# Attention and two feed-forward blocks on one core: the copies of the rounded q and k made by DMA, q's remainder made by POOL, first loads on two queues, new orders

## The chip, the core and the metric

The kernel runs on one core of a Trainium2 chip. The core has TensorE (PE, matrix products), VectorE (DVE), ScalarE (ACT), GpSimd (POOL) and SyncE (SP). Each engine works through its own instructions in the order in which they were written, and waits for the others by semaphores. PE reads its operands from on-chip memory (SBUF) and writes to a small accumulator memory (PSUM); DVE and ACT read both, POOL only SBUF. DMAs are issued by SP and by ACT. The metric is the device time of one execution, in microseconds (us).

## The reference

Four batches of eight heads, 576 positions, 64 elements in a head. Attention with a decay bias is followed by two feed-forward blocks; the change is in attention.

```python
scores = scale * np.matmul(q, k.transpose(0, 1, 3, 2))
cum = np.cumsum(np.maximum(s, 0.0), axis=-1)
bias = -(cum[:, :, :, None] - cum[:, :, None, :])
scores = np.where(causal, -1000000000.0, scores + np.minimum(bias, 0.0))
scores = scores - np.max(scores, axis=-1, keepdims=True)
attn = np.exp(scores)
attn = attn / (np.sum(attn, axis=-1, keepdims=True) + 1e-09)
attn_out = np.matmul(attn, v)
# x = attn_out, heads side by side; then
# block 1: relu(x @ w_in) = (u, v); v normalised over its elements;
#          (u * (w_spatial @ v + b_spatial)) @ w_out
# block 2: mixes of x with its shifted copy; sigmoid(xr @ w_r) * (relu(xk @ w_k)^2 @ w_v)
```

## The kernel before

The 32 heads are worked on in 16 pairs. Products of full precision are made of rounded parts: an operand is split into a rounded part and a remainder, and the products of these parts are added up. For q and k of a pair, `st_T` (line 360) does this: `first` casts the raw tile into the rounded part (items `wh` for q, `xh` for k), a second copy of that rounded part goes to other partitions (`ud` for q, `vd` for k), and `second` subtracts it from the raw tile for the remainder (`ul`, `vl`). Four tiles hold the result: W and X with the rounded parts on partitions 64 to 127, beside the bias rows and the maxima on partitions 0 to 3 and up; U and V with a rounded part on one half of the partitions and a remainder on the other. All are parts of one tile, so the profile calls them `big`; the raw q and k are `qk`.

`st_S` (line 393) multiplies W by X for approximate scores and takes their maxima on DVE (tile `s`, twelve products and twelve reductions for a pair, items `s0` to `s11`); `Ma` and `Mb` transpose the maxima on PE, copy them on ACT (`mt`) and send them by DMA into W. `st_E` (line 434) computes the scores with V, U and X, W (tile `ps`, items `e0` to `e9` and `ez`), exponentiates them on ACT, and blanks what lies above the diagonal on POOL (the selects of line 467). `st_V` (line 489) multiplies by v and by a column of ones (tile `pv`, items `a0` to `a4` and `b0` to `b4`); ACT copies the sums out (`fa`, `fb`, tile `pt`, line 516). The normalisation goes by DMA: `n1` sends the row of sums to a 128-partition tile (`r<-pt`), `n2` takes the reciprocal on DVE and sends it to DRAM (`rd<-r`), `n2b` loads it back onto 64 partitions (`rb<-rd`), and `n30` and `n31` multiply (line 538), one on DVE and one on POOL.

A step p (`step`, line 619) does E of pair p, V of pair p-1, S of pair p+1, T of pair p+2 and the end of the normalisation of pair p-2. The items of all these are carried out in the order of the table `ORDER` (line 549); items named in `LATE` are left for the next step. Each engine gets its instructions in that order. Between the items stand parts of the decoding of the later weights (`dL` loads, `dF` on ACT, `dD` on DVE and POOL, `dT` on ACT and POOL, `dS` stores). Each `ldq` and `ldk` loads q or k of a later pair. The tables `START` (line 606) and `TAIL1`, `TAIL2` (lines 878 and 882) do the same for pairs 0 to 2 and for the end of attention with the start of the first block. `ENGINE` (line 111) says which engine does an item (V is DVE, S is ACT, P is POOL), `QUEUE` (line 114) which DMAs go by ACT ("A"); the others go by SP. A DMA waits on SP until its source is ready, and all SP's later DMAs wait behind it.

Pairs 0 to 2 have entries of their own with the prefixes A, B and C; pairs 3 to 15, which steps 1 to 13 split, use the entries without a prefix:

```python
wh="S", xh="S", ud="S", vd="S", ul="V", vl="V"
```

Of the kernel before, what the change touches and what calls it, by code (L numbers as in the profile page):

```python
# [25 lines left out]
def tile_kernel(  # L26
# [560 lines left out]
    def ones():  # L587
# [3 lines left out]
        for t in VT:  # L591
# [15 lines left out]
    START = """ldk0 ldq0 lds ldk1 cx0 mask cw0 sums 0xh0 bases cx1 ldq1 sums2 0wh0 0ul0 dL 0wh1 rx00 dL 0ul1 augd pads0  # L607
               0xh1 pads1 1wh1 rx01 tiny 0ud0 s0 s5 0ud1 s3 1wh0 s10 dL 1ud0 cx2 dF s1 ldq2 cw1 1rows dD 1xh1 0vd0 1ud1
               s9 0vl0 dT s2 s8 2rows dF s4 1ul1 pads2 1xh0 s6 dL s11 1s0 s7 0vd1 1s4 dS 1ul0 2wh0 dF cw2 2wh1 dD Ma
               lv0 0vl1 1s6 2ud0 ldk2 1s3 1s10 lv1 e0 2ul0 Mb e1 e3 ltv0 2ul1 2xh0 2xh1 1vd1 1vd0 1s2 1s1 2vd1 e4 e2  # L610
               1vl1 1s7 ldq3 ldq4 1s9 2vl1 1s11 1s5 e5 1s8 ones 1Ma 1vl0 e7 ldk3 1Mb e6 2vd0 e8 e9 ez 2vl0 2ud1"""
# [266 lines left out]
    TAIL1 = """V1 e0 e3 va0 dF va1 e1 va2 WV e5 va3 va4 un2 vfa dT un2b vb0 vb1 e6 dD WS dF e4 dF dD vb2 vb3 dT vb4 vfb
               dF dT dT e2 un31 dS e8 g0 wa0 wa1 ez dF g0s dT vn1 dF wa2 e9 wa3 e7 g0c un30 wa4 dL wfa dL g1 wb0 wb1
               g0r WU wb2 dD wb3 dL wb4 vn2 dL wfb vn2b wn1 g1s dF dT g2 g3 dD g1c dS g2s dF g3s wn2 vn30 dS g1r dT dD  # L880
               g4 dL dF vn31 wn2b dD g3c g2c wn31 dD wn30"""
    TAIL2 = """dT dT dF dT q4 dD p1 dF g4s p0 dL dT q1 p0s g4c p1s g4r g3r B0 g2r dT dT q7 q3 q2 p2 p2s dL p3 p4 dD dF
               p4s q6 p3s q0 dD dS dS dS dF q5"""
# [195 lines left out]
```

## Time and profile before

| | |
|---|---|
| median of 3 runs | 686.35 us |
| lowest and highest run | 684.46 and 687.14 us |
| span of the profiled execution (no other time is given for it) | 684.9 us |
| busy: PE, DVE, ACT, POOL | 650.0, 504.3, 375.6, 341.8 us |
| mean of a step from 49.4 to 188.0 us (twelve steps) | 11.55 us |

The span is counted from the first to the last instruction of one profiled execution; it lies 1.45 us below the median of the runs. Start of attention, the steps and its tail take the first 263 us; after that PE works nearly without a gap. In a row of the profile, `out<-in` names the tile that is written and the tile that is read; a bracket at the end says how long the engine was idle before, and what ended that. A "q" behind an engine's name (SPq, ACTq) is its queue of DMA issues; such a row's duration is that of the issue, not of the transfer.

### The profile page before, as it was taken

The numbers are of one execution on the slowest core, as the hardware profiler recorded it, in microseconds if no ns is written. First come the engines' busy times: TensorE is split into PE (matmuls) and PEld (weight loads), VectorE is DVE, ScalarE is ACT, GpSimd is POOL, SyncE is SP. The second block draws the span as 40 slices with busy tenths as digits, with TensorE's granted clock in tenths as the row PEclk, the third lists the DMA queues.
The fourth block names the chain that finished last, engine by engine and source line by source line (L and its number), as shares of the span: only waits on it lengthen the run. The fifth ranks groups of instructions, "written<-read, shape, count | busy, mean of one in ns | idle before, by whom it ended". The sixth has DMA issues, their size and how long they took to land.

```text
span 684.9 us, 10966 instructions
## 1 busy us (share of the span) xinstructions
PE 650.0 (95%) x3640; PEld 558.0 (81%) x3640; DVE 504.3 (74%) x1038; ACT 375.6 (55%) x824; POOL 341.8 (50%) x490
## 2 busy tenths in 40 slices
PE   2599999999999979999999999999999999999998
PEld 1476666666757968998999999988989898898987
DVE  6878887878853687768858754479596877959773
ACT  5599999999975474575565453331423323142330
POOL 4445656565674646566567555442434344244430
PEclk9999999999999989999999999999999999999999
DMA  6645556564458627562364572721001010000101
GB/s 180 131 107 151 156 144 161 143 164 128 123 158 264 210 72 222 158 198 94 101 208 146 150 260 84 258 111 47 0 1 47 0 47 1 31 17 1 46 1 47
DMA packets 65065, 78.23 MB, mean 114 GB/s; under 512 B 28763, under 2 KB 45563, under 8 KB 64496
## 3 DMA queue, kind: packets, MB, share of 16 engines
q1 hardware_dynamic: 63674, 75.81, 37.0%
q10 hardware_dynamic: 1334, 1.72, 1.0%
q8 instruction: 28, 0.46, 0.3%
q14 instruction: 29, 0.24, 0.1%
HBM read 54.05 MB, written 21.79 MB: 111 GB/s over the span
## 4 chain that ended last, share of the span: by engine, by line
PE 78%; DMA 9%; ACT 7%; DVE 4%; issue 1%; POOL 0%; ACTq 0%; SPq 0%; DVEq 0%
PE mm L703 57%; PE mm L788 8%; PE pv L505 4%; DMA r<-pt 3%; PE ps L443 3%; DMA qk<-in_qk_dram 2%; ACT big L105 2%; ACT pt L516 2%; PE pv L502 2%; DMA rd<-r 1%; PE s L405 1%; ACT e L463 1%; PE pv L501 1%; DVE jk L411 1%; DMA big<-augd 1%
## 5 line engine op out<-in xcount | busy, mean ns | idle before, releaser
L703 PE MATMUL mm<-big 128*128 128x384 f32 (+2 forms) x1176 | 202.5, 332 | 0.0
L703 PEld LDWEIGHTS mm<-big 128*128 128x128 f32 x1176 | 191.3, 188 | 8.6
L703 PE MATMUL mm<-w,vb 128*128 128x512 f32 (+1 forms) x304 | 90.4, 381 | 0.0
L986 DVE TENSOR_TENSOR r<-r 128x384 f32<-128x384 f32 x48 | 53.7, 1119 | 46.6 <-ACT r L983 46.6
L443 PE MATMUL ps<-big 128*128 128x288 f32 (+3 forms) x320 | 84.0, 362 | 1.7 <-ACT e L463 0.8
L405 PE MATMUL s<-big 128*128 128x288 f32 (+3 forms) x192 | 61.9, 378 | 20.4 <-POOL big L108 12.3
L145 POOL TENSOR_TENSOR f<-f,raw 128x256 int32<-128x256 int32 x64 | 53.4, 834 | 43.9 <-DVE f L143 33.7
L411 DVE CUSTOM_DVE_ANT_0 jk<-s,mask 128x288 bf16<-128x288 f32 (+4 forms) x160 | 61.9, 429 | 16.2 <-PE s L405 13.9
L467 POOL TENSOR_SCALAR_AFFINE_SELECT e<-e 128x128 f32<-128x128 f32 x128 | 52.4, 419 | 42.0 <-ACT e L463 37.2
L443 PEld LDWEIGHTS ps<-big 128*128 128x128 f32 x320 | 55.3, 197 | 19.8 <-issue 12.1
L405 PEld LDWEIGHTS s<-big 128*128 128x128 f32 x192 | 36.3, 206 | 36.6 <-DVE mx L411 12.6
L463 ACT ACTIVATE e<-ps 128x288 f32<-128x288 f32 (+3 forms) x160 | 60.6, 418 | 8.5 <-PE ps L443 7.1
L703 PEld LDWEIGHTS mm<-w,vb 128*128 128x128 f32 x304 | 56.0, 188 | 11.2
L788 PE MATMUL mm<-ws,vb 128*128 128x288 f32 x384 | 59.3, 303 | 4.6 <-DVE ws L120 2.6
L505 PE MATMUL pv<-e,vp 128*65 128x448 f32 (+2 forms) x192 | 63.5, 436 | 0.0
L1006 DVE RECIPROCAL rr<-rr 128x512 f32<-128x512 f32 x18 | 60.4, 3353 | 0.6
L788 PEld LDWEIGHTS mm<-ws,vb 128*128 128x128 f32 x384 | 54.8, 194 | 5.6 <-DVE ws L120 3.4
L987 ACT CAST vb<-r 128x384 fp32r<-128x384 f32 x48 | 24.7, 515 | 56.9 <-DVE r L986 56.9
L729 POOL TENSOR_TENSOR gh<-mix,vb 128x384 fp32r<-128x384 f32 x24 | 25.5, 1070 | 52.3 <-ACT vb L728 49.7
L703 PE MATMUL mm<-gh,wo 128*128 128x288 f32 x256 | 51.3, 294 | 0.0
L729 POOL TENSOR_TENSOR big<-mix,big 128x384 fp32r<-128x384 f32 x24 | 25.9, 1083 | 47.4 <-ACT big L728 38.7
L120 DVE TENSOR_TENSOR big<-qk,big 64x1152 fp32r<-64x1152 f32 (+1 forms) x37 | 44.3, 1201 | 6.1 <-ACT big L105 4.9
(126 smaller groups left out, 1289.1 us busy)
## 6 DMA issues: line engine op xcount, KB each, us to landing
qk<-in_qk_dram SPq DMA_DIRECT2D x28, 288.0 KB
out_dram<-rr SPq DMA_DIRECT2D x17, 256.0 KB
rb<-rd SPq DMA_DIRECT2D x15, 288.0 KB
raw<-in_moe_w_in_dram SPq DMA_DIRECT2D x16, 256.0 KB
vp<-in_v_dram SPq DMA_DIRECT2D x16, 256.0 KB
raw<-in_moe_w_k_dram SPq DMA_DIRECT2D x16, 256.0 KB
raw<-in_moe_w_v_dram SPq DMA_DIRECT2D x16, 256.0 KB
big<-d_wk SPq DMA_DIRECT2D x8, 512.0 KB
```

The costliest lines, as they stand in the source:

```text
L145: nc.gpsimd.tensor_tensor(out=f, in0=f, in1=low, op=ALU.add)
L405: nc.tensor.matmul(out=ps[:, 0:kn], lhsT=W[g][:, h, 128 * i:128 * i + 128], rhs=X[g][:, x0:x0 + kn], start=True, stop=True,)
L411: nc.vector.tensor_tensor_reduce(out=jk[r0:128, 0:kn], in0=ps[r0:128, 0:kn], in1=mask[r0:128, m0:m0 + kn], scale=1.0, scalar=(dst if mid e ...
L443: nc.tensor.matmul(out=ps[:, o:o + b - a], lhsT=st[g][:, key0(h, 128 * j):key0(h, 128 * j) + 128], rhs=mv[g][:, h, 64 + a:64 + b], start=( ...
L463: nc.scalar.activation(out=e[:, o:o + n], in_=ps[:, 0:n], func=ACTF.Exp, scale=scale)
L467: nc.gpsimd.affine_select(out=d, in_=d, pattern=[[1, w]], base=0, channel_multiplier=-1, compare_op=ALU.is_ge, fill=0.0,)
L505: nc.tensor.matmul(out=pv[0:VW, 1, 448 - w:448], lhsT=lt, rhs=e[:, OFF[j]:OFF[j] + w] if j < 4 else es[p][:, w * h:w * h + w], start=False ...
L703: nc.tensor.matmul(out=ps, lhsT=x, rhs=y, start=(m == 0), stop=(m == n - 1))
L729: nc.gpsimd.tensor_tensor(out=dst[1][:, kc, :], in0=t, in1=dst[0][:, kc, :].bitcast(F32), op=ALU.subtract)
L788: nc.tensor.matmul(out=o, lhsT=x[:, sc, dd], rhs=y[:, sc, t], start=(sc == 0 and m == 0), stop=False)
L986: nc.vector.tensor_tensor(out=r, in0=r, in1=r, op=ALU.mult)
L1006: nc.vector.reciprocal(out=r, in_=r)
```

## The change

For pairs 3 to 15, `ud` and `vd` become DMAs on SP's queue. For q, ACT still casts into W and the DMA copies W's rounded part to U. For k, ACT now casts into V, on the partitions of the raw tile, and the DMA copies V's rounded part to X, which S reads; `vl` then needs the cast alone. `vd` is no longer in `LATE`, so it is issued in the step of the cast. q's remainder `ul` goes from DVE to POOL. k of pair 0 and q of pair 1 are loaded by SP's queue instead of ACT's, and the second maxima of pair 0 go by ACT's. `START`, `ORDER`, `TAIL1` and `TAIL2` are written in new orders; they hold the same items as before.

```diff
-    ENGINE = dict(... wh="S", xh="S", ud="S", vd="S", ul="V", vl="V", ...)
+    ENGINE = dict(... wh="S", xh="S", ud="D", vd="D", ul="P", vl="V", ...)
...
-    QUEUE = dict(lds="P", ldq0="A", ldk0="A", ..., ldq1="A", ldk1="A", ..., Mb="P", ...)
+    QUEUE = dict(lds="P", ldq0="A", ldk0="P", ..., ldq1="P", ldk1="A", ..., Mb="A", ...)
...
+        def moved(nm):
+            return ENGINE[f"{pre}{'ud' if nm == 'q' else 'vd'}{0 if len(heads) > 1 else ''}"] == "D"
+
         def first(nm, i, eng):
-            COPY[eng](hi(nm, i), raw(nm, i))
+            COPY[eng]((dup if nm == "k" and moved("k") else hi)(nm, i), raw(nm, i))
...
+        def again(nm, i, eng):
+
+            a, b = dup(nm, i), hi(nm, i)
+            if not moved(nm):
+                COPY[eng](a, b.bitcast(F32))
+            elif nm == "k":
+                nc.sync.dma_start(out=b.bitcast(F32), in_=a.bitcast(F32))
+            else:
+                nc.sync.dma_start(out=a.bitcast(F32), in_=b.bitcast(F32))
...
-                items[d + e] = lambda i=i, nm=nm, key=pre + d + e: COPY[ENGINE[key]](
-                    dup(nm, i), hi(nm, i).bitcast(F32))
+                items[d + e] = lambda i=i, nm=nm, key=pre + d + e: again(nm, i, ENGINE[key])
...
-    ORDER = """s4 s0 s3 wh zero lv s6 ul x1 e0 rows xh a0 dT n2 e1 a1 s1 n2b ltv s5 a2 s11 a3 dD vd x0 e2 s10 a4 s2 fa
+    ORDER = """x4 s4 wh x2 s0 ltv s3 dT e0 e1 s6 ul e2 dD lv n2 dL rows s1 a0 s2 a2 a1 x1 s11 xh s5 e4 a3 vd a4 n2b
...
-    LATE = "vd vl"
+    LATE = "vl"
```

SP's queue in the middle of the attention steps, from one rd to the next rb, before. Line 528 is rd, 534 rb, 124 a load of the decoding and 158 its store, 426 the maxima, 278 a load of q or k, 521 r, 357 the zeroed row, 284 v, 352 the bias rows.

```order
L528 DMA rd<-r_1417 128x9
L534 DMA rb<-rd 64x1152
L124 DMA raw<-in_moe_w_in_dram 128x256
L158 DMA d_wv<-hl_86 256x1x256
L426 DMA big<-mt 1x5x128
L278 DMA qk_137<-in_qk_dram 64x1152
L426 DMA big<-mt 1x5x128
L521 DMA r_1582<-pt 128x1x9
```

The same stretch of SP's queue after the change, from rd to r. Lines are 12 to 14 higher; 392 is the copy of k, 394 the copy of q.

```order
L540 DMA rd<-r_1419 128x9
L124 DMA raw<-in_moe_w_in_dram 128x256
L352 DMA big<-augd 3x1152
L392 DMA big<-big 64x1152
L546 DMA rb<-rd 64x1152
L357 DMA big<-big 1x16x80
L438 DMA big<-mt 1x5x128
L158 DMA d_wv<-hl_86 256x1x256
L394 DMA big<-big 64x2x576
L278 DMA qk_137<-in_qk_dram 64x1152
L438 DMA big<-mt 1x5x128
L533 DMA r_1584<-pt 128x1x9
```

Between rd and rb now stand a load, the bias rows and the copy of k; between rb and r stand six DMAs, among them the copy of q, where five stood.

POOL in the middle of the attention steps, before: the decoding (lines 120 and 145), the selects, the multiplication by rb (538), the selects of the last block (481, 484).

```order
L467 AFFINE_SELECT e<-e 128x128 x2
L120 TENSOR_TENSOR hl_86<-f,hl_86 128x256
L145 TENSOR_TENSOR f<-f,raw 128x256
L467 AFFINE_SELECT e<-e 128x128 x6
L538 TENSOR_TENSOR x_72<-pt,rb 64x576
```

POOL after the change, the same stretch, with q's subtraction as the line with `64x2x576`.

```order
L120 TENSOR_TENSOR hl_85<-f,hl_85 128x256
L479 AFFINE_SELECT e<-e 128x128
L120 TENSOR_TENSOR big<-qk_137,big 64x2x576
L479 AFFINE_SELECT e<-e 128x128
L145 TENSOR_TENSOR f<-f,raw 128x256
L479 AFFINE_SELECT e<-e 128x128 x6
L550 TENSOR_TENSOR x_72<-pt,rb 64x576
```

q's subtraction stands between the first two selects of a step, behind the decoding's subtraction and ahead of its addition.

## Rows read from the trace of the kernel before

**Rows 1.** The page, first part: busy us, share of span, instructions.

```profile
PE 650.0 (95%) x3640; PEld 558.0 (81%) x3640; DVE 504.3 (74%) x1038; ACT 375.6 (55%) x824; POOL 341.8 (50%) x490
```

**Rows 2.** By step: us, busy PE, PEld, DVE, ACT, POOL; clock, DMA share, GB/s.

```profile
118.40:130.00 11.60, 11.12 (x61) 7.84 (x60) 9.34 (x32) 11.18 (x23) 6.67 (x14) 1.00 0.54 145
...
sum 138.60, PE 134.19 PEld 94.69 DVE 116.12 ACT 132.50 POOL 80.81; mean PE 11.18 PEld 7.89 DVE 9.68 ACT 11.04 POOL 6.73
```

**Rows 3.** Chain of waits: start us, us, what. PE's rate without disturbance, two places.

```profile
123.28 0.75 PE pv L502 x2
...
299.47 1.58 PE mm L788 x12
```

**Rows 4.** Chain of waits in two steps.

```profile
116.27 3.73 DMA r<-pt
120.02 0.21 DVE r L526
...
127.25 0.64 ACT pt L516
...
128.11 1.83 DMA r<-pt
```

**Rows 5.** SP's queue in order of time: start us, us of issue, line.

```profile
116.27 0.51 SPq L521 DMA_DIRECT2D r<-pt  x1
...
120.31 0.35 SPq L528 DMA_DIRECT2D rd<-r  x1
122.69 0.47 SPq L534 DMA_DIRECT2D rb<-rd  x1
...
128.11 0.51 SPq L521 DMA_DIRECT2D r<-pt  x1
```

**Rows 6.** Groups by shape, eight steps: count | busy, mean ns | idle before.

```profile
L120 DVE TENSOR_TENSOR big<-qk,big 64x1152 fp32r<-64x1152 f32 x17 | 23.3, 1373 | 2.1 <-ACT big L105 1.8
L105 ACT CAST big<-big 64x1152 fp32r<-64x1152 f32 x16 | 18.4, 1153 | 0.4
...
L411 DVE CUSTOM_DVE_ANT_0 jk<-s,mask 128x448 bf16<-128x448 f32 x16 | 9.3, 619 | 0.0
...
L538 DVE TENSOR_TENSOR x<-pt,rb 64x576 f32<-64x576 f32 x8 | 6.1, 762 | 3.5 <-DMA rb<-rd 3.3
```

**Rows 7.** Line 120 by engine: ns min/median/max, first and last start, shapes.

```profile
L120 POOL TENSOR_TENSOR big<-qk,big x1: 1407/1407/1407, 16.9 to 16.9; 64x576 fp32r<-64x576 f32 x1
```

**Rows 8.** In order of time, POOL's two, then DVE's two beside them.

```profile
106.72 1.04 POOL L467 TENSOR_SCALAR_AFFINE_SELECT e<-e 128x128 f32<-128x128 f32 x1 [0.50 <-ACT e L463]
...
115.24 1.92 POOL L538 TENSOR_TENSOR x<-pt,rb 64x576 f32<-64x576 f32 x1
...
106.25 1.35 DVE L120 TENSOR_TENSOR big<-qk,big 64x1152 fp32r<-64x1152 f32 x1 [0.22 <-ACT big L105]
...
115.13 0.75 DVE L538 TENSOR_TENSOR x<-pt,rb 64x576 f32<-64x576 f32 x1 [1.08 <-DMA rb<-rd]
```

**Rows 9.** Chain of waits: a load of 64 rows, 288 KB, to its landing.

```profile
91.17 4.10 DMA qk<-in_qk_dram
```

**Rows 10.** Start of the kernel in order of time, POOL, DVE, ACT, PE.

```profile
5.18 0.72 POOL L108 TENSOR_SCALAR big<-qk 64x576 fp32r<-64x576 f32 x1 [1.50 <-DMA qk<-in_qk_dram]
...
7.01 0.75 DVE L335 TENSOR_TENSOR big<-e,big 32x576 fp32r<-32x576 f32 x1
...
9.00 0.67 ACT L105 CAST big<-qk 64x576 fp32r<-64x576 f32 x1 [2.40 <-DMA qk<-in_qk_dram]
9.42 1.32 ACTq L342 DMA_DIRECT2D big<-big  x1
...
12.26 3.40 PE L405 MATMUL s<-big 128*128 128x288 f32 x8 [12.26 <-POOL big L108]
```

**Rows 11.** By stretch, columns as in group 2: end of attention.

```profile
200.00:220.00 20.00, 18.64 (x89) 12.92 (x89) 5.99 (x17) 10.04 (x24) 11.50 (x23) 1.00 0.83 260
...
240.00:260.00 20.00, 15.40 (x92) 14.37 (x91) 16.18 (x29) 14.62 (x33) 8.49 (x10) 0.83 0.23 69
```

More of the change, by code (lines that the diff above doesn't have):

```diff
@@ L110, in tile_kernel @@
     COPY = {"V": vcopy, "S": scopy, "P": pcopy}
-    ENGINE = dict(n30="V", dH="S", dO="P", n31="P", xe0="P", xe1="V", xe2="P", xe3="P", xe4="P", gl0="P", gl1="V", gl2="P", gl3="V", cw0="V", cx0="S", cw1="D", cx1="S", cw2="V", cx2="D", bs="V", N130="V", N131="V", N140="P", N141="V", N150="V", N151="V", wh="S", xh="S", ud="S", vd="S", ul="V", vl="V", Awh0="S", Axh0="P", Aud0="P", Avd0="S", Aul0="V", Avl0="P", Awh1="S", Axh1="V", Aud1="P", Avd1="S", Aul1="V", Avl1="V", Bwh0="S", Bxh0="S", Bud0="P", Bvd0="S", Bul0="V", Bvl0="V", Bwh1="P", Bxh1="S", Bud1="S", Bvd1="P", Bul1="V", Bvl1="V", Cwh0="P", Cxh0="S", Cud0="S", Cvd0="V", Cul0="V", Cvl0="V", Cwh1="S", Cxh1="S", Cud1="S", Cvd1="P", Cul1="V", Cvl1="V", ph0="S", pl0="V", ph1="S", pl1="V", ph2="S", pl2="V", ph3="S", pl3="V", ph4="S", pl4="V")
-    QUEUE = dict(lds="P", ldq0="A", ldk0="A", ltq0="A", ltk0="P", ldq1="A", ldk1="A", rx00="A", rx01="P", augd="A", Ma="P", Mb="P", n13="A", d13="P", b13="P", n14="P", d14="A", b14="P", n15="A", d15="A", b15="A")
+    ENGINE = dict(n30="V", dH="S", dO="P", n31="P", xe0="P", xe1="V", xe2="P", xe3="P", xe4="P", gl0="P", gl1="V", gl2="P", gl3="V", cw0="V", cx0="S", cw1="D", cx1="S", cw2="V", cx2="D", bs="V", N130="V", N131="V", N140="P", N141="V", N150="V", N151="V", wh="S", xh="S", ud="D", vd="D", ul="P", vl="V", Awh0="S", Axh0="P", Aud0="P", Avd0="S", Aul0="V", Avl0="P", Awh1="S", Axh1="V", Aud1="P", Avd1="S", Aul1="V", Avl1="V", Bwh0="S", Bxh0="S", Bud0="P", Bvd0="S", Bul0="V", Bvl0="V", Bwh1="P", Bxh1="S", Bud1="S", Bvd1="P", Bul1="V", Bvl1="V", Cwh0="P", Cxh0="S", Cud0="S", Cvd0="V", Cul0="V", Cvl0="V", Cwh1="S", Cxh1="S", Cud1="S", Cvd1="P", Cul1="V", Cvl1="V", ph0="S", pl0="V", ph1="S", pl1="V", ph2="S", pl2="V", ph3="S", pl3="V", ph4="S", pl4="V")
+    QUEUE = dict(lds="P", ldq0="A", ldk0="P", ltq0="A", ltk0="P", ldq1="P", ldk1="A", rx00="A", rx01="P", augd="A", Ma="P", Mb="A", n13="A", d13="P", b13="P", n14="P", d14="A", b14="P", n15="A", d15="A", b15="A")
     def queue(key):
@@ L548, in tile_kernel @@
     late = {}
-    ORDER = """s4 s0 s3 wh zero lv s6 ul x1 e0 rows xh a0 dT n2 e1 a1 s1 n2b ltv s5 a2 s11 a3 dD vd x0 e2 s10 a4 s2 fa
-               e4 x2 e5 dL s8 e3 s7 b0 ud dS vl Ma dF b1 e8 s9 e7 e6 ldk n30 n31 b2 b3 Mb b4 fb ez n1 e9 x3 ldq x4""".split()
-    LATE = "vd vl"
+    ORDER = """x4 s4 wh x2 s0 ltv s3 dT e0 e1 s6 ul e2 dD lv n2 dL rows s1 a0 s2 a2 a1 x1 s11 xh s5 e4 a3 vd a4 n2b
+               zero fa s8 e5 e3 s10 e9 Ma b0 vl s7 s9 e8 dS ud e7 n31 b2 dF ldk b3 ez Mb b1 n30 b4 fb x3 n1 x0 e6
+               ldq""".split()
+    LATE = "vl"
     def run(*stages):
@@ L606, in tile_kernel @@
                   for key in ("cw0", "cx0", "cw1", "cx1", "cw2", "cx2")})
[L607 to L611, printed above, removed]
+    START = """tiny cw0 pads1 lds ldq0 sums ldk0 cx0 0xh0 bases 0wh0 pads0 ldk1 cx1 dL sums2 rx00 mask ldq1 1wh1
+               rx01 0ul0 0ud0 dL 0xh1 0wh1 0ul1 s0 cx2 ldq2 s5 s6 0ud1 augd dF dL 1rows s1 s3 0vd0 1ud1 1xh1 dD cw1
+               s7 s8 lv1 s10 0vd1 0vl0 2wh0 s2 s4 s9 dT 1wh0 dF 1ul1 2wh1 1xh0 s11 dS 0vl1 1s0 1s6 dD cw2 Ma ldk2
+               1s3 1ud0 dL 1vd0 1s10 e0 dF e3 pads2 2xh0 1ul0 e1 2xh1 1s2 2ud0 2ul1 Mb 2ul0 ldq4 1vd1 2rows 2vd1
+               lv0 1vl1 1s7 e4 ltv0 ones e2 1s1 1s4 1s8 1s5 ldq3 e5 1s9 2vd0 1Ma e7 1s11 e8 2vl0 2vl1 e9 1Mb 1vl0
+               2ud1 ez ldk3 e6"""
     for nm in START.split():
@@ L877, in tile_kernel @@
     })
[L878 to L883, printed above, removed]
+    TAIL1 = """e0 dF V1 va0 va3 va2 e1 va1 WV un2 va4 e5 vfa dT dF vb0 e9 vb3 vb1 dD un2b dT vb2 ez e4 vb4 dF vfb
+               e6 e8 dT dT un30 WS g0 wa0 e2 dD e3 un31 wa1 dF vn1 g0s dT e7 wa2 wa3 wa4 dL dF dS dL g0c wfa vn2 g1
+               g0r WU wb0 wb1 dL wb3 wb2 g1s wb4 dF wfb dF dT wn1 g2 vn2b g3 g1c dD dD dF g2s wn2 g3s dD dS g1r g4
+               wn2b vn31 vn30 dL dF dT g3c dS dD g2c wn31 dD dL wn30"""
+    TAIL2 = """dT dD dT g4s dD dT p0 dF dT p0s q3 p1 dL q4 g4c g2r p1s g4r q0 dT g3r q7 B0 p2 p2s p3 p4 p3s q2 p4s
+               dF q6 dS dL dF q1 dD dF dS dS q5 dT"""
     for nm in TAIL1.split():
```

## The prediction

> **What bounds the kernel now.** I read the page first. PE is busy for 95% of the span [rows 1], but its ends are modelled, so I looked for the stretches in which it does less than it could. The busy times by stretch show two: the first 40 us, and the attention steps from 49 to 188 us. Those are twelve steps in 138.6 us, 11.55 us each, and one step has 11.04 us of ACT work, 9.68 of DVE and 6.73 of POOL [rows 2]. ACT is full to 96%, so it is the first thing that sets a step.
>
> How low could PE go? Twelve products of 288 columns take 1.58 us where nothing disturbs them, 0.457 ns a column; a value product of 448 columns takes 0.75 us, 1.674 ns a column [rows 3]. A step has 6,400 columns of the scores that are exponentiated (E) and 3,200 of the scores for the maxima (S) at the first price, 3,200 of values and 256 of transposes at the second: 4.39 + 5.36 + 0.43 = 10.2 us. That is PE's floor; 1.35 us a step is lost.
>
> The chain of waits tells the rest. From 116 to 128 us it runs: the DMA r<-pt that takes 3.73 us, DVE's reciprocal at 120.02, DVE and PE work, ACT's copy of the second head's sums at 127.25, and the next r<-pt at 128.11 [rows 4]. So there is a second limit beside ACT: the normalisation goes through DMAs, and DVE, which works in order, stands at the reciprocal until the first has landed. SP shows the whole ring: r at 116.27, rd at 120.31, rb at 122.69, the next r at 128.11 [rows 5]. DVE's multiplication by rb also waits, 3.3 us over eight steps [rows 6].
>
> **The change part by part.**
>
> 1. *ACT loses two copies a step.* Each is 1.153 us [rows 6]. 11.04 - 2 x 1.153 = 8.73 us a step. ACT no longer sets the step.
>
> 2. *DVE loses q's subtraction*, 1.373 us [rows 6]: 9.68 - 1.37 = 8.31 us. k's stays.
>
> 3. *POOL gains it.* The trace has one POOL subtraction of this kind, 64x576 in 1.407 us [rows 7]; twice that is 2.81 us for 64x1152 (an estimate). 6.73 + 2.81 = 9.54 us a step, so POOL goes from the idlest engine to one that is nearly full. Its selects are used half a step to a step later, which covers a lag of a few us.
>
> 4. *POOL and DVE hold each other up.* At 115.24 POOL began a multiplication that took 1.92 us; the same shape took 1.41 elsewhere. DVE had begun a two-input operation at 115.13, which ended at 115.88. At 106.72 a POOL select began that took 1.04 us; DVE's subtraction ran from 106.25 to 107.60, and the select ended 0.16 us later [rows 7, 8]. So one waits for the other to end. The subtraction that moves held POOL for 1.37 us a step; now it can hold DVE for 2.81. In the new order it stands on POOL beside DVE's three decode operations, and the reciprocal stands right behind these. Bounds: from 0 (DVE's three come first; no gain, since POOL's selects have their cover) to 2.81 us a step (POOL's comes first each time). I take 0.3, about one meeting of the size of rows 8 (0.5 us) in every second step, because the two go by turns there, and keep both ends.
>
> The Trainium skill, "SBUF — State Buffer", section "Who interferes with whom", states this as a rule that speaks against the change: a DVE instruction with two SBUF inputs and a GpSimd instruction that reads SBUF exclude each other for a whole instruction, whichever starts first. By that rule a collision costs DVE up to the full POOL subtraction, where sums per engine would cost nothing: the step would be 10.7 us by the sums, 674 us in all, and 12.5 us with half of the subtraction in DVE's way, 697 us in all. The two meetings of rows 8 agree with the rule.
>
> 5. *Two DMAs a step go onto SP's queue*, 288 KB each. An issue takes some 0.5 us of SP, and SP has waits to absorb it; twelve issues become fourteen. A load of that size and row length landed 4.10 us after its issue [rows 9]. The copy of k is needed by the first score product of the next step. k's cast ends on ACT some 4.5 us into the step (an estimate: q's and k's cast at 1.15, four or five short operations ahead of it at about 0.4), the DMA is issued by 5.6 and lands by 9.7, 1.3 us before an 11.0 us step ends. That is its cover; what it slips beyond that, PE waits. The copy of q has a whole step. Bytes: 1.7 MB a step now, 2.3 after, 206 GB/s over 11.0 us; 260 GB/s was moved from 200 to 220 us [rows 11]. So it fits, but a DMA waits more often behind another: 0 to 1 us on the ring r, rd, rb.
> Queued behind k's copy, which waits for ACT, stand rb, the zero row and the maxima, so DVE and POOL, which wait for rb, wait for it too. As rb waits for rd to land anyway (2.4 us between their issues [rows 5]), the raw load, the rows and k's copy lie in that gap.
>
> 6. *The new order* puts DVE's three decode operations ahead of the reciprocal where q's subtraction stood. The chain of rows 4, worked out anew: copy 0.64 and 0.2 to r's issue (both from 127.25 to 128.11), r 3.73, reciprocal 0.21, two score reductions until PE gets a buffer, 1.1 (the widest is 0.62 [rows 6]), then PE's remaining work of the step: 4,640 columns at 0.457 ns, 1,600 + 256 at 1.674 ns, 5.2 us. Sum 11.1 us. In every second step r took only some 1.8 us in the chain (1.83 at 128.11 [rows 4]), and PE's floor holds, 10.2 to 10.4. Mean 10.7; with 0.3 from point 4, **11.0 us a step** against 11.55.
>
> 7. *First loads.* ACT's first cast of q waited until 9.00 us for its load, issued behind k's on the same queue; the rows' DMA stood behind it at 9.42, and PE began at 12.26. k's load, issued first, was there at 5.18 [rows 10]. With q first on ACT and k on SP, the rows' DMA waits only for DVE's sums, ready at 7.76, and goes out 1.6 us earlier. DVE is busy for most of the rest of the start, so later reorderings give little. Bounds 0 to 3 us; I take 1.5.
>
> 8. *The tail's orders.* PE loses 4.6 us between 240 and 260, with a mean granted clock of 0.83 of the full 2.4 GHz [rows 11], in a run of small ACT, DVE and POOL steps that are only reshuffled. Nothing in the trace says which way; between -3 and +3, taken as 0.
>
> **Sum.** The changed copies lie in thirteen steps: 13 x (11.55 - 11.0) = 7.2, and 1.5 from the start: 8.7 off the profiled span of 684.9 us gives 676.2. The median of the runs is 1.45 above that span: **678 us**.
>
> **The rivals.**
> - *PE's floor is reached.* r's landing and the port cost nothing more, as ACT's late copies were what delayed the sums: 10.3 us a step, 13 x 1.25 + 1.5 = 17.8, 668.6 us. For it: ACT is at 96%. Against it: DVE's waits for DMAs in rows 4 and 6, which are not ACT's.
> - *The ring of r, rd and rb stays as long as it is.* 0.4 us more on it from DMAs behind one another, and a step takes 11.5: 13 x 0.05 + 1.5, 684 us. For it: in rows 5 the time from r to r is 11.84 us, and six issues besides r itself now stand between rb and the next r where five stood.
> - *Slower: POOL's subtraction gets in ahead of DVE's decode.* It decides whether POOL's operation starts before DVE's third one. Then DVE stands for up to 2.81 us ahead of the reciprocal, half of it on average, 1.4: 11.1 + 1.4 = 12.5 us a step, 13 x 0.95 = 12.4 more, less 1.5: 697 us. For it: rows 8, and the rule named above. Against it: the two take turns there, and POOL has three shorter operations to do first.
>
> **How the numbers follow.** Forecast 0.45, floor 0.15, ring unchanged 0.24, slower 0.16. One measurement can tell 0.5%, 3.4 us, from no change: below 682.9 is faster, above 689.8 slower. Faster: 0.40 of the forecast's, 0.15 of the floor's and 0.02 of the ring's, 0.57. Within: 0.25. Slower: 0.15 of the last and 0.03 of the ring's if the tail goes wrong too, 0.18. The range takes in the floor case with its start (667) and reaches into the slower case up to 693: less than 0.2 is left out. The likeliest case alone, with start and tail at their bounds, is 673 to 683.
>
> **What would show it.** In the steps from 49 to 188 us: ACT at some 8.7 us a step, POOL at 9.5, two DMA issues more, and a step of 11.0. Point 4 shows as DVE decode operations that last until POOL's subtraction ends; point 5 as PE waiting at the first score product for big<-big; the ring as idle time of DVE before the reciprocal and before the multiplication by rb; point 7 as PE's first product near 10.7 us. The prediction is wrong if a step is under 10.5 or over 11.5 us, or if the time moves outside attention by more than 4 us.

## The result and the profile after

The changed kernel takes 691.15 us against 686.61 us measured beside it (twelve runs each), a ratio of 1.0054 with an interval of 1.0028 to 1.0080: half a per cent slower. The profiled execution has a span of 689.4 us; before it was 684.9. Step times come from one profiled execution each, and runs of one kernel differ by some 1% (the changed kernel's lie from 686.5 to 694.4 us): of the experiments below, e8's profile is of its slowest run (695.8 us, median 690.3) and e9's of its fastest (678.0, median 683.7).

| stretch | before | after | difference |
|---|---|---|---|
| first score product begins | 12.26 us | 10.88 us | -1.4 |
| first reciprocal of the steps | 50.18 us | 51.89 us | +1.7 |
| mean of the next eleven steps | 11.58 us | 12.19 us | +0.61 each, +6.8 |
| end of the tail: PE begins the first product behind batch 0's spatial part | 263.05 us | 267.78 us | +4.7 |

A step is counted from one reciprocal of DVE to the next; the twelfth stands 8.5 us later than before, so some 3.8 us come back in the tail. The page of the changed kernel, busy time of each engine, the main DMA queue, and the costliest group with a wait (count, busy, mean, idle time ahead of it):

```profile
PE 646.6 (94%) x3640; PEld 558.9 (81%) x3640; DVE 495.3 (72%) x1025; ACT 344.8 (50%) x798; POOL 387.5 (56%) x503
...
q1 hardware_dynamic: 66816, 84.07, 43.9%
...
L417 PE MATMUL s<-big 128*128 128x448 f32 (+3 forms) x192 | 69.3, 413 | 30.7 <-DMA big<-big 22.6
```

PE does the same 3640 products. The 22.6 us that its score products wait for a DMA big<-big are not all of the steps: 10.9 us are the kernel's beginning (the first product at 10.88 us; before, it waited 12.3 us for POOL there), 2.9 a wait at 20 us, and 8.8 belong to the steps. These 8.8 are new. The queue's packets take 43.9% of the sixteen DMA engines' span; in the profile of before it was 37.0%. By step (columns as in [rows 2]), one step and the sum over eleven:

```profile
112.90:125.50 12.60, 10.83 (x58) 8.12 (x56) 8.42 (x30) 8.91 (x21) 10.33 (x15) 0.90 0.94 194
...
sum 134.10, PE 120.89 PEld 88.18 DVE 94.83 ACT 96.84 POOL 108.84; mean PE 10.99 PEld 8.02 DVE 8.62 ACT 8.80 POOL 9.89
```

Against [rows 2]: ACT 8.80 us a step where it had 11.04, DVE 8.62 for 9.68, POOL 9.89 for 6.73, just as the parts of the change say. But a step became longer and the DMA engines, at 0.54 in the step shown before, are at 0.94 here. The mean granted clock of this step is 0.90; what stood ahead of that is told below. The groups of eight steps, which answer to [rows 6, 7]:

```profile
L120 POOL TENSOR_TENSOR big<-qk,big 64x1152 fp32r<-64x1152 f32 x8 | 21.2, 2650 | 0.7
...
L550 POOL TENSOR_TENSOR x<-pt,rb 64x576 f32<-64x576 f32 x8 | 15.4, 1931 | 13.1 <-DMA rb<-rd 7.3 <-ACT e L475 4.2 <-ACT pt L528 1.6
...
L550 DVE TENSOR_TENSOR x<-pt,rb 64x576 f32<-64x576 f32 x8 | 6.0, 751 | 17.8 <-DMA rb<-rd 17.8
...
L143 DVE SCALAR_TENSOR_TENSOR f<-raw,g 128x256 int32<-128x256 int32 x7 | 5.4, 773 | 0.6
...
L417 PE MATMUL s<-big 128*128 128x192 f32 x16 | 4.6, 290 | 6.6 <-DMA big<-big 5.4 <-DMA big<-mt 1.2
```

The multiplications by rb wait 17.8 us on DVE, where [rows 6] had 3.3, and 7.3 us on POOL. The chain of waits through two steps shows who is late (start, length, what):

```profile
101.39 2.42 DMA rd<-r
...
103.83 0.49 SPq L546
...
104.37 4.76 DMA big<-big
...
109.17 0.65 PE s L417 x3
...
115.05 0.53 SPq L546
...
115.95 5.73 DMA big<-big
...
121.82 0.63 PE s L417 x3
```

In both steps it goes from rb's issue (line 546) through a DMA big<-big issued right behind it, 4.76 and 5.73 us, to PE's first score product (109.17 and 121.82). SP's queue names that DMA; it answers to [rows 5]:

```profile
113.12 0.36 SPq L540 DMA_DIRECT2D rd<-r  x1
...
114.43 0.51 SPq L392 DMA_DIRECT2D big<-big  x1
115.05 0.53 SPq L546 DMA_DIRECT2D rb<-rd  x1
115.95 0.57 SPq L357 DMA_DIRECT2D big<-big  x1
...
120.56 0.55 SPq L533 DMA_DIRECT2D r<-pt  x1
```

Line 392 is the copy of k, line 357 the zero row of W. PE's wait at 121.82 is for the zero row: a few kilobytes, issued at 115.95 behind rb, landing 5.7 us later. In the kernel before nobody waited for that line. In the changed kernel (us, times):

```profile
  PE s L417: 8.8, 8
  PEld s L417: 3.3, 3
```

This is the reading that the chain by names alone would have hidden: the copy of k and the zero row have the same name.

Such a wait can be followed by more than its own length. PE's row at the end of the second one:

```profile
121.82 0.63 PE L417 MATMUL s<-big 128*128 128x192 f32 x3 [1.76 <-DMA big<-big]
```

PE had done next to nothing from 120 to 122 us (0.24 us busy), and from 123 to 126 us the granted clock is 0.50 of full speed, 1.2 GHz. It is the one such stretch in the steps of the changed kernel (the wait of 1.86 us that ends at 73.21 us has none behind it); in the steps of the kernel before there is none.

### The profile page after: what moved, and what is told of

It reads as the page before. It is cut to its first block, busy times and chain, and to the rows that moved or that the text cites. A ratio compares the mean times of both kernels' runs of the same rounds, so it can differ in the third digit from the quotient of the medians.

```text
span 689.4 us, 11078 instructions
## 1 busy us (share of the span) xinstructions
PE 646.6 (94%) x3640; PEld 558.9 (81%) x3640; DVE 495.3 (72%) x1025; ACT 344.8 (50%) x798; POOL 387.5 (56%) x503
## 3 DMA queue, kind: packets, MB, share of 16 engines
q1 hardware_dynamic: 66816, 84.07, 43.9%
## 4 chain that ended last, share of the span: by engine, by line
PE 81%; DMA 10%; DVE 3%; ACT 2%; issue 1%; POOL 1%; SPq 0%; ACTq 0%; DVEq 0%; POOLq 0%
PE mm L717 56%; PE mm L802 8%; PE pv L517 5%; PE ps L455 5%; DMA big<-big 4%; DMA r<-pt 3%; PE s L417 3%; PE pv L514 2%; DMA big<-mt 1%; PE pv L513 1%; DMA rd<-r 1%; DMA augd<-big 1%; PE mm L804 1%; PE mm L803 1%; ACT big L105 1%
## 5 line engine op out<-in xcount | busy, mean ns | idle before, releaser
L417 PE MATMUL s<-big 128*128 128x448 f32 (+3 forms) x192 | 69.3, 413 | 30.7 <-DMA big<-big 22.6
L455 PE MATMUL ps<-big 128*128 128x288 f32 (+3 forms) x320 | 70.6, 332 | 5.1 <-DMA big<-mt 4.1
L423 DVE CUSTOM_DVE_ANT_0 jk<-s,mask 128x320 bf16<-128x320 f32 (+4 forms) x160 | 63.9, 427 | 15.3 <-PE s L417 14.2
L145 POOL TENSOR_TENSOR f<-f,raw 128x256 int32<-128x256 int32 x64 | 55.2, 863 | 23.2 <-DVE f L143 9.0
L517 PE MATMUL pv<-e,vp 128*65 128x192 f32 (+2 forms) x192 | 61.9, 433 | 0.7 <-POOL e L479 0.7
L479 POOL TENSOR_SCALAR_AFFINE_SELECT e<-e 128x128 f32<-128x128 f32 x128 | 50.9, 418 | 15.3 <-ACT e L475 14.0
L455 PEld LDWEIGHTS ps<-big 128*128 128x128 f32 x320 | 51.9, 197 | 7.9 <-DMA big<-mt 4.6
L1004 POOL TENSOR_TENSOR big<-r,vb 128x384 fp32r<-128x384 f32 x30 | 30.4, 1013 | 32.0 <-ACT vb L1001 26.5
```

What stands on the lines that cost most here:

```text
L145: nc.gpsimd.tensor_tensor(out=f, in0=f, in1=low, op=ALU.add)
L417: nc.tensor.matmul(out=ps[:, 0:kn], lhsT=W[g][:, h, 128 * i:128 * i + 128], rhs=X[g][:, x0:x0 + kn], start=True, stop=True,)
L423: nc.vector.tensor_tensor_reduce(out=jk[r0:128, 0:kn], in0=ps[r0:128, 0:kn], in1=mask[r0:128, m0:m0 + kn], scale=1.0, scalar=(dst if mid e ...
L455: nc.tensor.matmul(out=ps[:, o:o + b - a], lhsT=st[g][:, key0(h, 128 * j):key0(h, 128 * j) + 128], rhs=mv[g][:, h, 64 + a:64 + b], start=( ...
L479: nc.gpsimd.affine_select(out=d, in_=d, pattern=[[1, w]], base=0, channel_multiplier=-1, compare_op=ALU.is_ge, fill=0.0,)
L517: nc.tensor.matmul(out=pv[0:VW, 1, 448 - w:448], lhsT=lt, rhs=e[:, OFF[j]:OFF[j] + w] if j < 4 else es[p][:, w * h:w * h + w], start=False ...
```

## The experiments

Ratios are to the kernel before, run beside each; "step" is the mean of the eleven steps after the first reciprocal, from the profiled execution. In runs of the kernel before's steps (its own profile and three of the runs below) that mean is 11.58 to 11.77 us.

### Undoing one part in the steps

The first theory was that PE waits because the copies are late. Each of four runs sets back one entry of the engine table:

```diff
-ud="D", vd="D", ul="P"
+ud="D", vd="S", ul="P"    # e1: k's copy back on ACT
+ud="S", vd="D", ul="P"    # e2: q's copy back on ACT
+ud="S", vd="S", ul="P"    # e3: both
+ud="D", vd="D", ul="V"    # e4: q's subtraction back on DVE
```

> The changed kernel with k's second copy back on ACT in the steps; q's copy stays a DMA, POOL keeps q's subtraction, orders and first loads stay. Theory (the DMA engines: two 288 KB copies a step fill them to 0.88, the copy of k lands 5.5 to 7 us after its issue and PE waits for it): PE's waits at the first score product (25.9 us in all) go, the DMA share of the steps falls from about 0.88 to about 0.78, ACT goes to 9.5 us a step; a step is 11.6 us instead of 12.19, the whole 683 to 685 us against 691.2 of the changed kernel. Rival 'POOL's subtraction holds DVE up': the step stays near 12, the whole at 689 to 691. Rival 'the new order itself': 690 to 692, since only the place where the wait shows would move.

Measured: 1.0047 (1.0027 to 1.0067), step 11.98 us. PE's wait for the zero row fell to 0.6 us, and the time stayed. PE now waits at the second head's first value product for ACT's copy of the sums, 6.9 us in ten steps, where the changed kernel had none:

```profile
L513 PE MATMUL pv<-e,vp 128*65 128x128 f32 x40 | 8.1, 285 | 6.9 <-ACT pt L528 6.9
```

> The changed kernel with q's second copy back on ACT in the steps; k's copy stays a DMA. Theory (load on the DMA engines): q's copy has a whole step of cover, nobody waits for it, but the engines carry 1.8 us less a step, so k's copy lands 1 to 2 us sooner, and rb and k's next load too: a step of 11.8, the whole 686 to 688 us. Rival 'the place of k's copy alone' (SP's order and its waits, not the load): nothing gained, 690 to 692. Rivals 'POOL's subtraction' and 'the new order': 690 to 692.

Measured: 1.0046 (1.0021 to 1.0071), step 12.11 us. PE's wait for the zero row stayed, 11.1 us: k's copy is enough for it.

> The changed kernel with both second copies back on ACT in the steps: what remains of the change is POOL's subtraction, the new orders and the first loads. Theory: no PE wait for a copy, DMA share near 0.65, but ACT at 11.0 us a step again, so a step of 11.5 to 11.6 as before; start 2 us worse, tail 3.8 us better than before: 683 to 684 us. Rival 'POOL's subtraction': steps still over 12, 689 to 692. Rival 'the new order': likewise 689 or more.

Measured: 1.0084 (1.0054 to 1.0114), step 12.15 us. So the theory missed three times: taking the copies away from the DMA engines wins nothing as long as ACT gets them back. All three times lie where the rival 'the new order' had put them. But the landings changed. From rb's issue on SP to the multiplication on DVE that waited for it:

```profile
104.68 0.50 SPq L546 DMA_DIRECT2D rb<-rd  x1
```

```profile
108.22 0.75 DVE L550 TENSOR_TENSOR x<-pt,rb 64x576 f32<-64x576 f32 x1 [1.17 <-DMA rb<-rd]
```

3.54 us here; in the changed kernel 115.05 to 121.16, 6.11 us (the first in SP's queue above, the second in a row under point 4 below). Over all steps in which DVE waited (from the issue of rb or r on SP to the DVE instruction that waited for it):

| | rb, median (range), cases | r, median, cases | DMA share, 60 to 180 us |
|---|---|---|---|
| before | 3.80 (3.71 to 3.94), 9 | 3.71, 4 | 0.57 |
| changed | 5.53 (3.97 to 6.15), 11 | 3.99, 10 | 0.87 |
| e3, both copies on ACT | 3.82 (3.50 to 4.18), 11 | 2.20, 12 | 0.62 |
| e9, copies cut (below) | 3.82 (3.54 to 4.64), 12 | 2.66, 9 | 0.69 |

> The changed kernel with q's subtraction back on DVE in the steps; both copies stay DMAs. Theory (DMA load): nothing better, DVE gets 1.4 us a step more beside its waits for rb: 690 to 693 us. Rival 'POOL's subtraction holds DVE up': the step falls back towards 11.5, 683 to 686 us. Rival 'the new order': 690 to 692.

Measured: 1.0230 (1.0181 to 1.0279), step 13.20 us. In the new order with the copies as DMAs, the move of the subtraction is worth some 12 us; it isn't what costs.

### The orders

```diff
 # e5: ORDER of the kernel before in the changed kernel (LATE stays "vl")
 # e6: the changed kernel with ud="S", vd="S", ul="V"
 # e7: the kernel before with ul="P"
 # e8: zero in its old place
-x4 s4 wh x2 s0 ... a4 n2b zero fa
+x4 s4 wh zero x2 s0 ... a4 n2b fa
```

> The changed kernel with the step order of before; both second copies stay DMAs, POOL keeps q's subtraction, first loads, start and tail stay as changed. Theory (the new step order costs the time: the zero row stands behind rb on SP there, rb's issue is far back, chains through r and rb are longer): a step falls from 12.19 to 11.2 to 11.5 us, the whole 679 to 684 us, PE without waits for the zero row. Rival 'the two copies fill the DMA engines': a step stays at 12 or more, 689 to 692 us, with PE waiting for k's copy. Rival 'POOL's subtraction': likewise 12, 689 to 692.

Measured: 1.0271 (1.0242 to 1.0300), step 13.51 us. A miss for every theory. With the copies in the old order PE waits for the row of maxima instead, the E product behind it:

```profile
L455 PE MATMUL ps<-big 128*128 128x288 f32 x70 | 22.1, 383 | 9.9 <-DMA big<-mt 9.0 <-ACT big L105 0.9
```

> The changed kernel with both second copies back on ACT and q's subtraction back on DVE in the steps: of the change only the orders and the first loads remain. Theory (the step order): a step of 12.2 to 12.6 us, so 691 to 697 us. Rival 'POOL's subtraction': without it the step is 11.5 to 11.6, 683 to 685 us. Rival 'the DMA copies': already out by the runs with k's copy or both on ACT, which stayed at 12.0 to 12.15 us a step.

Measured: 1.0331 (1.0302 to 1.0360), step 13.64 us, worse than either theory. The new order with the old engines (e6) and the old order with the new engines (e5) both lose more than the whole change: an order and the engines of its items belong together, as far as these runs go.

> The kernel before with one edit: q's subtraction goes from DVE to POOL in the steps. Theory (the order is at fault, not POOL): a step of 11.4 to 11.6 us, the whole 683 to 687 us against 686 to 689 of before. Rival 'POOL's subtraction holds DVE up': a step of 12, 690 to 694 us, with DVE's two-input operations longer by 0.3 us and more.

Measured: 1.0010 (0.9994 to 1.0027), step 11.86 us. In the old order POOL's subtraction alone costs nothing that can be measured.

> The changed kernel with one item of the step order moved: the zero row (W[3:4]) is copied right behind q's cast, ahead of the reciprocal and of rb on SP, where it stood in the kernel before. Theory (PE waits for the zero row, which is issued behind rb and lands 5 to 6 us later): PE's 12 us of waits for it go, a step falls from 12.19 to about 11.5, the whole 683 to 687 us. Rival 'k's copy itself comes late': PE's waits at the first score product move to that copy, 689 to 692 us.

Measured: 1.0028 (1.0006 to 1.0051), step 12.43 us. The interval overlaps that of the changed kernel, so no gain is shown. Nobody on PE waits for the zero row any more, but its waits went to the next late things: 2.3 us (and 1.4 of weight loads) to k's copy, as the rival said, and 7.4 us of score products of 288 columns to DVE, which has to free a buffer and itself stands 28.5 us in ten steps for rb. So the wait for the zero row is not what the change costs by itself:

```profile
L417 PE MATMUL s<-big 128*128 128x288 f32 x39 | 16.3, 419 | 7.4 <-DVE mx L423 7.4
...
L550 DVE TENSOR_TENSOR x<-pt,rb 64x576 f32<-64x576 f32 x10 | 7.5, 752 | 28.5 <-DMA rb<-rd 28.5
```

### The bytes of the copies

The second theory: what the copies move fills the DMA engines, and the small DMAs on which the step hangs (r, rd, rb, the zero row, the maxima) land later. Two runs take the bytes away and leave issues, places and waits; two put bytes into the kernel before.

```diff
 # e9: the steps' copies cut to 36 of 576 columns a head
-nc.sync.dma_start(out=b.bitcast(F32), in_=a.bitcast(F32))
+nc.sync.dma_start(out=b[:, :, 0:36].bitcast(F32), in_=a[:, :, 0:36].bitcast(F32))
 # e14: cut to 4 of 64 partitions: b[0:4], a[0:4]
 # e10, in the kernel before: c0 ahead of n2b, c1 behind ud and dS
+def spare_copy():
+    nc.sync.dma_start(out=spare, in_=mask[0:64, None, 0:S].broadcast_to([64, 2, S]))
 # e17: the same with in_=qk[0, 0:64]
```

> The changed kernel with both copies of the steps cut to 36 of 576 columns a head; their issues, their places on SP and their waits stay, so this leaves out 15/16 of what they move and part of the result is not computed. Theory (the bytes of the two copies: the small DMAs of the ring, r, rd, rb, the zero row and the maxima, land late behind them): DMA share of the steps back to 0.6, DVE's and POOL's waits for rb (37 us in eleven steps) down to 10 or less, a step of 11.0 to 11.4 us, the whole 677 to 681 us. Rival 'the new order and its places on SP': a step stays at 12.0 to 12.2, 689 to 692 us.

Measured: 0.9914 (0.9886 to 0.9941), step 11.41 us. Against the changed kernel 0.0140 of the time comes back: 9.6 us, give or take 2.6. The waits for rb fell, though not as far as expected, and those for the zero row nearly went (60 to 180 us, ten steps; the changed kernel had 22.9 us in the first group and 8.9 in the second, 7.7 of them for the zero row):

```profile
L550 DVE TENSOR_TENSOR x<-pt,rb 64x576 f32<-64x576 f32 x10 | 7.5, 752 | 15.5 <-DMA rb<-rd 15.5
...
L417 PE MATMUL s<-big 128*128 128x192 f32 x21 | 5.7, 274 | 2.0 <-DMA big<-big 2.0
```

> The changed kernel with both copies of the steps cut to 4 of 64 partitions, whole rows; issues, places and waits stay, 15/16 of the copied data is left out, so part of the result is not computed. Theory (what the copies occupy on the DMA engines is the whole loss): DMA share of the steps near 0.55 to 0.6, under the 0.69 of the run with short rows, DVE's waits for rb below 16 us in eleven steps, a step of 10.9 to 11.2, the whole 673 to 679 us. Rival 'the ring r, rd, rb is long by its order alone': a step of 11.4 and 681 to 684 us, as with the short rows.

Measured: 0.9916 (0.9889 to 0.9943), the same gain, step 11.79 us. The rival for this run holds: without the bytes the time is 683 us, not 678. Some of the wait for rb (19.3 us in eleven steps here) belongs to the new order, and PE still waits 5.3 us for a DMA big<-big. The two runs also tell bytes from packets: e9 moves no fewer packets on the main queue than the changed kernel (67648 to 66816), e14 does (64164), and both gain the same.

> The kernel before with two more 288 KB copies a step on SP, from a constant tile in SBUF to a tile that nobody reads, one ahead of rb and one behind q's copy on ACT; nothing else changes. Theory (the bytes make the ring late): DMA share of the steps from 0.57 to about 0.85, DVE's waits for rb and r from 7 us to over 20 us in eleven steps, a step of 12 us and more, the whole 692 to 700 us. Rival 'the engines are the bound and DMAs are covered': a step of 11.6, 686 to 690 us.

Measured: 1.0127 (1.0099 to 1.0155), step 12.80 us: 8.7 us for bytes that nobody reads. The wait that grew isn't the one for rb, as had been expected (5.9 us on DVE in the steps, 4.6 before), but DVE's for r (8.5 us, 2.5 before) and, on PE, again the maxima:

```profile
L443 PE MATMUL ps<-big 128*128 128x288 f32 x75 | 22.9, 376 | 8.3 <-DMA big<-mt 8.3
```

> The kernel before with two more 288 KB DMAs a step at the places of the run with spare copies (697.1 us), but loads from DRAM to the tile that nobody reads, not copies within SBUF. If a copy within SBUF is what is dear: DMA share 0.62 to 0.68 in the steps, the whole 688 to 691 us. If the bytes alone count: 0.73 as with the spare copies, 695 to 699 us.

Measured: 1.0161 (1.0123 to 1.0199), step 12.65 us. Loads of the same size from DRAM cost as much within the intervals. So it's not that the copies lie within SBUF; what the two runs have in common is twice 288 KB a step on the DMA engines. Two things besides the bytes are in these times, and no run takes them apart: each DMA more takes SP 0.5 to 0.65 us to issue (in e9 and e14 these issues stay, so their gain is free of that), and the granted clock is 0.96 and 0.97 from 60 to 180 us where the kernel before has 1.00; e10 has three stretches at 0.50 in it, e17 two, the changed kernel and e14 one, e9 none. From 60 to 180 us (busy PE, PEld, DVE, ACT, POOL; clock, DMA share, GB/s), first the changed kernel, then e3, e9, e10 and e17:

```profile
60.00:180.00 120.00, 108.72 (x595) 79.59 (x596) 85.54 (x300) 86.70 (x199) 98.53 (x140) 0.99 0.87 191
```

```profile
60.00:180.00 120.00, 109.60 (x594) 78.57 (x593) 82.20 (x300) 108.93 (x220) 93.34 (x139) 1.00 0.62 144
```

```profile
60.00:180.00 120.00, 113.88 (x636) 83.92 (x635) 89.49 (x319) 91.00 (x211) 105.31 (x148) 1.00 0.69 156
```

```profile
60.00:180.00 120.00, 109.77 (x563) 76.54 (x564) 88.21 (x288) 103.84 (x204) 60.51 (x120) 0.96 0.73 181
```

```profile
60.00:180.00 120.00, 109.25 (x569) 77.06 (x569) 89.80 (x291) 105.30 (x208) 59.66 (x123) 0.97 0.74 182
```

### Another queue, one copy alone

```diff
 # e13: both copies of the steps
-nc.sync.dma_start(
+nc.scalar.dma_start(
 # e16: order, start and LATE of before, tails of after, ud="D" alone
 # e18: as e16, with ud moved
-n2b ltv s5 ... b0 ud dS vl
+n2b ud ltv s5 ... b0 dS vl
```

> The changed kernel with the two copies of the steps issued from ACT's queue, at the same places of the order, instead of SP's. Theory 'one queue' (the small DMAs stand behind the copies on SP's queue): r, rd, rb, the zero row and the maxima land as early as with the cut copies, a step of 11.4, the whole 680 to 684 us. Theory 'the DMA engines' (all 16 are shared by both queues): the small DMAs are as late as before, a step of 12.0 to 12.4 and 689 to 694 us.

Measured: 1.0211 (1.0162 to 1.0260), step 13.02 us. The small DMAs on SP's queue didn't overtake the copies on the other queue: rb landed after 5.18 us in the median (4.77 to 7.01), and PE's wait for the zero row's line was 16.5 us where the changed kernel had 8.8. In the group of the first score products, ten steps:

```profile
L417 PE MATMUL s<-big 128*128 128x192 f32 x19 | 5.7, 297 | 15.6 <-DMA big<-big 15.4 <-issue 0.2
```

This speaks for the shared engines and against the one queue. The Trainium skill says the same in "DMA: Bandwidth & Descriptors", section "Issuing engines are not separate DMA queues": DMAs from whichever engine run on the same sixteen DMA engines. This run agrees, and is worse beyond that; the cause of this rest was not tried.

> The kernel before with the new tail orders (alone: 685.7 us) and q's second copy of each step as a DMA, at its old place in the old step order; k's copy and both subtractions stay where they were. If one copy fits into the DMA engines and ACT's 1.15 us a step count: a step of 11.2, 680 to 683 us. If the copy makes the ring and the maxima late as the two of the run with spare copies did, half as much: a step of 11.8, 687 to 691 us.

Measured: 1.0092 (1.0062 to 1.0123), step 12.26 us. Against the tails alone (e11 below, 0.9948) one copy costs 9.9 us although ACT has 1.15 us a step less to do, a miss on the dear side. PE waits 6.6 us in eleven steps for the maxima.

> The run with the new tails and q's copy alone as a DMA (695.2 us), with that DMA's place moved from ahead of the first maxima's row to right behind rb. If the small DMAs behind the copy pay (the maxima's row, for which PE waited 6.6 us in eleven steps): PE's waits for it go, 684 to 688 us. If the bytes count wherever they go: 693 to 697 us, with rb or r or the next load late instead.

Measured: 1.0064 (1.0044 to 1.0083), step 12.31 us. That is at the lower edge of what was expected if the bytes count wherever they go, and the intervals of e16 and e18 overlap. PE's wait for the maxima fell to 4.3 us. That the place of the copy decides is not shown; why one copy costs as much as two in other places stays open.

### The start and the tail

```diff
 # e11: the kernel before with TAIL1 and TAIL2 of after
 # e12: the kernel before with START and QUEUE of after
 # e15: as e12, with
-Mb="A"
+Mb="P"
```

> The kernel before with the two new tail orders and nothing else. If the new tails are worth what the traces of the two kernels show from the last step on (3.8 us): 683 to 685 us where before has 687 to 688. Rival 'the gain came from the later arrival of the last steps' (work that waited in the tail had had time to be done): 686 to 689 us.

Measured: 0.9948 (0.9928 to 0.9967), 685.7 us: the new tails are worth 3.6 us by themselves. Of the versions here that leave nothing out it is the fastest.

> The kernel before with the new start order and the queues of the first loads, and nothing else. Theory (the start's second maxima go out on ACT's queue and land late): first score product near 10.9 instead of 12.26, but the first value product near 39 instead of 37.1, the whole 688 to 691 us. Rival 'the start's loss comes from the three first copies by DMA and the step order behind it': first value product at 36 to 37, 685 to 688 us.

Measured: 1.0034 (1.0017 to 1.0051), first value product at 37.77 us, first reciprocal at 52.48 (before: 37.1 and 50.18). The start costs 2.3 us.

> The kernel before with the new start order and first-load queues, as in the run that did this alone (690.8 us), but the second maxima of pair 0 go out on SP's queue again. Theory (that DMA, issued from ACT's queue behind its work, is the start's loss): 687 to 689 us, first value product at 36 to 37 us. Rival 'the start order itself': 690 to 692 us.

Measured: 1.0030 (1.0014 to 1.0045). The suspicion falls: the queue of the second maxima isn't the loss. Which reordering is stays open.

## Why the prediction was wrong

The terms, in us, each measured by the run that isolates it (688 us times its difference from 1, or from another run):

| term | predicted | measured | from |
|---|---|---|---|
| steps without what the copies move | -7.2 | -4.7 (±2.6) | e9, less start and tail |
| bytes of the copies | 0 (allowed: 0 to 1 us a step on the ring) | +9.6 (±2.6), 0.74 a step | changed kernel less e9 |
| start | -1.5 | +2.3 | e12 |
| tail | 0 (±3) | -3.6 | e11 |
| sum | -8.7 | +3.6 | the changed kernel: +3.7 (1.9 to 5.5) |

The first row is what e9 leaves: -5.9, less 2.3, plus 3.6. It takes the parts as adding up, which no run shows, and by it the sum is the changed kernel's own ratio again, so its agreement is no check. By the prediction's own sign, a step over 11.5 us, it failed: a step took 12.19. That 691 lies in its range (up to 693) is luck: the upper part of the range was there for POOL in DVE's way, which is not what happened.

**Points 1 to 3 were right**, within 0.4 us a step. ACT, DVE and POOL came out at 8.80, 8.62 and 9.89 us a step; 8.73, 8.31 and 9.54 were said. POOL's subtraction takes 2.65 us, 2.81 was the estimate.

**Point 4 was right in size.** The meetings are there. DVE's k subtraction and POOL's addition, which takes 0.74 us undisturbed, and ahead of them POOL's subtraction:

```profile
115.89 1.35 DVE L120 TENSOR_TENSOR big<-qk,big 64x1152 fp32r<-64x1152 f32 x1
...
121.16 0.75 DVE L550 TENSOR_TENSOR x<-pt,rb 64x576 f32<-64x576 f32 x1 [2.95 <-DMA rb<-rd]
```

```profile
112.93 2.65 POOL L120 TENSOR_TENSOR big<-qk,big 64x1152 fp32r<-64x1152 f32 x1
...
115.91 1.94 POOL L145 TENSOR_TENSOR f<-f,raw 128x256 int32<-128x256 int32 x1
```

The addition ends 0.61 us behind DVE's subtraction, 1.94 us in all. DVE's third decode operation has a mean of 0.77 us where it had 0.43, a third of a microsecond a step, as taken. The slower rival, POOL in DVE's way for 697 us, isn't what happened: with the move undone (e4) the time rises, and in the kernel before the move alone costs nothing (e7). The row at 121.16 is the multiplication that waited 2.95 us for rb.

**Point 5 failed, and with it the sign.** The step that failed is "so it fits": it compared bytes, 206 GB/s wanted, 260 seen in [rows 11], allowed 0 to 1 us on the ring for DMAs behind one another, and put nothing of it into the sum. The runs show 9.6 us in its place, 0.74 us a step, inside what it had allowed. Compared by the engines' time instead of GB/s, the steps are nearly full: with the copies the share is 0.87 at 191 GB/s, where [rows 11] had 0.83 at 260. Worked out from the queue's packets: 43.9% of 689.4 us less 38.1% of 691.9 us (e3's page) is 39.0 us for 26 copies, 1.5 us of all sixteen engines for one. [Rows 2] had the share at hand, 0.54 in an 11.6 us step, 6.3 us: with two copies of 1.5 us it is 9.3 of 11.0, 0.84. The 1.5 was not known then; at [rows 2]'s own rate, 145 GB/s at 0.54, a copy is 1.1 us (an estimate) and the share 0.77, still well above 0.54. Then r and rb, which stand one behind the other in a step's loop, land later: rb by 1.7 us, r by 1.8 against the same order with the copies on ACT (e3), though only by 0.3 against the kernel before. The prediction also costed the copy of k by its own landing and cover (1.3 us), and put the price there; PE in fact waited for the zero row that the new order had put behind rb. Point 5 names that row among what is queued behind the copy, but says of it only that DVE and POOL wait; that PE reads the row is not in it. What each of the late DMAs (r, rb, the zero row, the maxima) costs alone no run shows; e8 took the zero row's wait away and gained nothing that can be told from noise.

**Point 6** gave the step 11.0 us. Without the bytes it is 11.41 and 11.79 in the two profiles, and 11.58 to 11.77 in those with the steps of before, so the profiles settle nothing here. By the timed runs it is 0.36 us a step (4.7 over 13, give or take 0.2) below the kernel before, which does not exclude the 0.55 that was said. What the profiles do show is a term that was left out: the sum of point 6 let the loop end at r, while DVE in the new order waits for rb as well, 15.5 us in ten steps even with the copies cut.

**Point 7 was half right.** The first score product came at 10.88 us (10.7 was said). The gain did not last to the first reciprocal. By the chain, PE soon waits for other DMAs of the start:

```profile
10.88 1.04 PE L417 MATMUL s<-big 128*128 128x288 f32 x3 [10.88 <-DMA big<-big]
```

```profile
29.06 4.17 DMA big<-mt
```

PE's waits for a DMA big<-mt in the first 50 us went from 0.5 to 4.1 us. "DVE is busy for most of the rest of the start, so later reorderings give little" was the wrong step: from 1.4 us ahead at the first score product the kernel came to 1.7 behind at the first reciprocal.

**Point 8** left ±3 us open and took 0; the tails give 3.6 (±1.3). The stretch from 240 to 260 us, which answers to [rows 11], has 3.2 us more of PE work, at a mean granted clock of 0.91 instead of 0.83 (the same in the stretch 4.7 us later, which lies as far ahead of the tail's end):

```profile
240.00:260.00 20.00, 18.56 (x124) 17.78 (x124) 18.77 (x34) 14.87 (x33) 10.98 (x12) 0.91 0.26 83
```

The nearest rival was the ring that stays as long as it is, 684 us, with the right mechanism (DMAs behind one another) at 0.4 us a step; 691 would have taken 0.9, 7 us more over 13 steps.

**What moving the copies is worth.** Put on ACT in the new order the two copies cost 0.0170 of the time against the run with cut copies (e3 less e9), 11.7 us; as DMAs 9.6 us. So the move traded one price for nearly the same; the difference of e3 and the changed kernel (0.0030) is within their intervals.

## What to carry to other kernels

Cost a DMA in time on the sixteen engines, not in GB/s: take the DMA share of the step, add what the nearest DMAs of its size take, and where it rises much (here from 0.57 to 0.73 or 0.87, for 9 to 11 us), expect the small DMAs in the step's loop to land later before anything is taken as gained. When an order is rewritten, list for each moved DMA who reads what it writes, however small; PE came to wait for the row of zeros, not for the 288 KB beside it, though taking that wait away (e8) was not enough to gain. Try an order only together with the engines that its items run on: parts of this change without the rest cost 2.3 to 3.3% (e4 to e6), though one move alone in the old order cost nothing (e7).

## What was not expected of the hardware

By the time of its packets, a DMA of 288 KB on 64 partitions holds all sixteen engines for about 1.5 us (an estimate from the queue's share), 200 GB/s, whether it copies within SBUF (e10: 41.5% of 696.3 us less 37.0% of 684.9 us, over 26, is 1.4) or loads from DRAM (e17: 41.9% of 697.3 us, 1.5). At a DMA share of 0.87 a DMA that lands 3.8 us after its issue at 0.57 takes 5.5, and a row of a few kilobytes 4.8 and 5.7 in the two steps shown. A second queue for the large ones didn't shield the small ones (e13: rb 5.2 us). Each stretch of the steps at a granted clock of 0.50, 1.2 GHz, in the changed kernel, e10 and e17 stands behind a wait of PE for a DMA of 1.4 to 2.4 us, and lasts some 3 to 4 us, so a late DMA can cost more than the wait: in the changed kernel two value products of 448 columns take 1.70 us at 124.27, where two took 0.92 at 115.84. Not each such wait is followed by one (1.86 us at 73.21 us).
